# Linear attention and a squared-ReLU layer on one core: aligned tiles, u from one row, the bonus moved by SBUF transfers, new engine orders

## The chip, the core and the metric

The kernel runs on one core of one Trainium2 chip. The core has five engines with instruction streams of their own: TensorE (PE; its weight loads are listed as PEld), VectorE (DVE), ScalarE (ACT), GpSimd (POOL) and SyncE (SP), which here only issues DMAs. Tiles lie in SBUF, 128 partitions wide; PE writes to PSUM, eight banks of 2 KB in each partition. Sixteen DMA engines move data. The metric is the device time of one execution in microseconds (us), as the median of several runs.

## The reference

A linear attention with a decayed state for 4 batches, 8 heads, 768 positions and 48 channels, then a layer with squared ReLU on 3072 tokens of 384 channels:

```
for t in range(S):
    cur = np.einsum('bhd,bhe->bhde', u[None] * kt, vt)
    y[:, :, t] = np.einsum('bhd,bhde->bhe', rt, state + cur)
    state = wt[:, :, :, None] * state + np.einsum('bhd,bhe->bhde', kt, vt)
...
x = attn_out.transpose(0, 2, 1, 3).reshape(B * S, H * D)
h = x @ w_in                 # 384 x 2048
r = np.maximum(h, 0.0)
return ((r * r) @ w_out)     # 2048 x 384
```

The term with u, the bonus, touches one position alone: it adds to y at t the row v at t, times the sum over d of r, u and k.

## The kernel before

The 3072 tokens are cut into 12 steps of 256 (three to a batch). A step's tile holds 128 partitions with two neighbouring positions each (j = 0, 1) for all 8 heads; the 128 partitions are two chunks (c = 0, 1) of 64. Each step goes through these operations, each a small function:

- **Loads** (`ld`): w, r, k, v of a step, 384 KB each, in runs of 384 bytes. The weights come as eight pieces of 768 KB and are cast to bf16 (`cast`). u is loaded as 128 equal rows (`load_u`, L188).
- **Decays**: `ww_` multiplies the two positions' w (L243), `lw_` takes the logarithm on ACT (L247), `cum_` sums along the positions on PE (L284 to L287), `exp_` and `ac_` go back on ACT (L291, L298). `rw_` and `kw_` make further products on DVE or POOL (L256, L260).
- **Decayed r and k**: `rd_` on DVE (L305); their transposes by PE (`tr_`, L314) and a copy (`rkt_`, L323) in steps 0 to 3, by DMA (`dtr_`, L326) from step 4 on.
- **Inside a chunk**: `p_` multiplies r and k (L341), `pm_` masks on DVE (L351 or L354), `y_` multiplies by v (L394).
- **State**: `su_` (L371), `ts_` (L379, L381) and `sn_` on POOL (L386); `yc_` adds the state's part to y (L394).
- **Bonus**: `ku_` and `qp_` on POOL form u k r (L264, L269), `q_` sums it on DVE (L273), `vq_` on POOL multiplies v by it and writes bf16 (L277). `yq_` (L411) adds it to y on PE: a 64-row product with the matrix `spread` for each of the two positions j and the two chunks c. The rows of y in PSUM are ordered by (j, position in the chunk) with the chunk in the free dimension, those of `vq` by (c, position) with j in the free dimension, so the product moves rows.
- **y on to the layer**: `ysb_` copies y from PSUM to bf16 on ACT or DVE (L436). Its transpose `xT` is made by PE and a copy (`yt_`, L444, `xt_`, L449) in steps 0 to 5, by DMA (`dyt_`, L453) from step 6 on.
- **Layer**: `m1_` (L464), eight groups of six matmuls a step; `rl_` (ReLU, on ACT L473 or DVE L475); `sq_` (square, L481 or L483); `m2_` (L489), two halves of 16 matmuls, in four pieces each; `os_` scales out of PSUM (L496, L498); `store` (L502).

What sets the order of the work is the text `ORDER` (L17): one word for each operation, with its step, for some the PSUM bank after a colon and the engine after an equals sign (A, V, G for ACT, DVE, POOL). The program is issued in this order, and each engine, and SP's DMA queue, executes its own instructions in it. `warm_` words are products without use at the start (L506).

PSUM is held as two double banks `att` for the attention part, two banks `bk` for `m2_` and transposes, and two banks `m1_bank` for `m1_`. Tiles in SBUF come from rotating pools; `half_ones` has 4 bytes in a partition, `q` 64, and a head's part of `r_raw` and `k_raw` 576.

Of the kernel before, what the change touches and what calls it, by code (L numbers as in the profile page):

```python
# [17 lines left out]
ld.0.w warm_.16.0 ld.1.w ld.0.k ld.0.u ld.0.r ld.1.r ww_.1=V ww_.0=V ld.1.k ld.0.v lw_.0 lw_.1 kw_.0=V  # L18
cum_.1:0 ku_.0 cum_.0:1 ld.0.i warm_.13.0 ac_.0 ac_.1 rw_.0=V exp_.0 qp_.0 ld.1.v exp_.1 rd_.0.0 rd_.0.1
tr_.0.0:0 ld.1.i warm_.1.1 rw_.1=V ld.2.w rkt_.0.0=A tr_.0.1:1 q_.0 ku_.1 rkt_.0.1=A ld.3.i rd_.1.0  # L20
p_.0.0:mm v_.0=A kw_.1=V qp_.1 warm_.2.0 rd_.1.1 su_.0:1 ld.2.k tr_.1.0:0 pm_.0.0 ts_.0.0=A tr_.1.1:1
rkt_.1.0=A p_.0.1:0 sn_.0.0 ld.2.r pm_.0.1 rkt_.1.1=A vq_.0 v_.1=A ts_.0.1=V y_.0:0 q_.1 cast.i.0=A sn_.0.1
p_.1.1:mm yq_.0 pm_.1.1 yc_.0 vq_.1 p_.1.0:1 ysb_.0=A ld.2.i warm_.3.0 pm_.1.0 ld.0.o cast.i.1=A yt_.0:0
su_.1:0 xt_.0=V y_.1:1 ts_.1.0=V ld.1.o yq_.1 ww_.2=V m1_.0.2:0 sn_.1.0 m1_.0.3:1 rl_.0.2=A yc_.1 cast.i.3=V
rl_.0.3=A m1_.0.1:0 lw_.2 ts_.1.1=V ld.2.o ysb_.1=A m1_.0.6:1 sq_.0.1=V ld.2.v cum_.2:0 rl_.0.1=V rl_.0.6=A
yt_.1:1 exp_.2 m1_.0.7:1 xt_.1=V rw_.2=V m1_.0.0:0 rl_.0.7=A kw_.2=V rl_.0.0=A rd_.2.0 m1_.1.0:1 cast.i.2=G
ac_.2 m1_.1.7:0 sq_.0.3=A rl_.1.0=V tr_.2.0:0 rd_.2.1 ku_.2 ld.3.o rl_.1.7=A m1_.1.5:1 sq_.0.0=A ld.3.w
m1_.0.5:0 rl_.1.5=V ld.3.r tr_.2.1:1 cast.o.0=V sn_.1.1 rl_.0.5=A m1_.1.4:1 rkt_.2.0=V m1_.0.4:0 rl_.1.4=A
rkt_.2.1=A rl_.0.4=V qp_.2 m1_.1.1:1 sq_.1.2=V m2_.0.0.0:0 cast.o.1=A m1_.1.2:0 ld.3.k pp_.2:10 rl_.1.2=A
m2_.0.0.1 rl_.1.1=A pm_.2.1 v_.2=G sq_.0.2=A m1_.1.3:0 cast.o.2=G ld.3.v q_.2 m1_.1.6:1 m2_.0.1.0:1 pm_.2.0  # L30
rl_.1.6=A vq_.2 m2_.0.1.1 cast.o.3=A ld.4.w rl_.1.3=V su_.2:0 m2_.0.1.2 ww_.3=G sq_.1.0=A ld.4.r m2_.0.0.2
lw_.3 m2_.0.1.3 sq_.1.1=A cum_.3:1 os_.0.1=V ld.4.k m2_.0.0.3 rw_.3=V exp_.3 m2_.1.0.0:1 ts_.2.0=V kw_.3=G
sq_.1.3=A rd_.3.0 m2_.1.0.1 ld.5.r sn_.2.0 m2_.1.0.2 ac_.3 os_.0.0=A rd_.3.1 m2_.1.0.3 v_.3=A ku_.3
store.0.1 tr_.3.0:0 os_.1.0=V yy_.2:01 ww_.4=V qp_.3 ld.4.v rkt_.3.0=V lw_.4 tr_.3.1:1 ysb_.2=A m2_.1.1.0:0
rkt_.3.1=V ld.5.k ts_.3.0=A cum_.4:1 rw_.4=V sn_.3.0 yt_.2:1 exp_.4 m2_.1.1.1 xt_.2=V ac_.4 ld.5.w m2_.1.1.2
rd_.4.0 kw_.4=G m1_.2.1:1 ts_.3.1=V dtr_.4.0 ku_.4 m1_.2.0:0 rd_.4.1 rl_.2.1=A rl_.2.0=A m1_.2.5:1 q_.3
dtr_.4.1 pp_.3:01 sn_.3.1 rl_.2.5=A m1_.2.3:0 pm_.3.1 ld.6.w vq_.3 m2_.1.1.3 rl_.2.3=A pm_.3.0 m1_.2.2:1
v_.4=A qp_.4 m1_.2.6:0 ld.7.w sq_.2.0=A rl_.2.2=V yy_.3:10 rl_.2.6=V ld.5.v sq_.2.1=A ww_.5=V kw_.5=G
os_.1.1=A m1_.2.4:1 rw_.5=V ld.7.r ysb_.3=A m1_.2.7:0 lw_.5 yt_.3:1 ts_.4.0=V rl_.2.4=A m2_.2.0.0:0 ld.6.k
xt_.3=A sn_.4.0 sq_.2.2=V m2_.2.0.1 ku_.5 cum_.5:0 store.1.1 m2_.2.1.0:1 ac_.5 q_.4 exp_.5 m1_.3.1:1  # L40
ts_.4.1=V rl_.2.7=A m2_.2.1.1 rd_.5.0 rl_.3.1=A m1_.3.7:0 ww_.6=G sq_.2.3=A rd_.5.1 m2_.2.1.2 dtr_.5.0
# [12 lines left out]
cum_.8:1 rw_.8=G sq_.5.0=A m1_.5.2:1 ld.10.w m2_.4.0.0:1 rl_.5.2=V rl_.5.4=A ww_.9=G m2_.4.0.1 exp_.8
ts_.7.1=V qp_.7 m1_.5.7:0 ac_.8 rd_.8.0 sq_.5.1=A m1_.5.6:1 rd_.8.1 m2_.4.0.2 dtr_.8.0 rw_.9=G m2_.4.0.3
# [34 lines left out]
def kernel(  # L90
# [17 lines left out]
    C = 128  # L108
# [458 lines left out]
```

## Time and profile before

| What | us |
|---|---|
| median of 3 runs (lowest, highest) | 189.27 (189.17, 189.53) |
| the profiled execution: span | 186.7 |
| busy PE, DVE, ACT, POOL | 177.0, 125.8, 125.1, 104.9 |
| L464 (`m1_`), 576 matmuls | 74.3 |
| L489 (`m2_`), 384 matmuls | 71.9 |
| L394 with `spread` (`yq_`), 48 matmuls | 6.0 |
| `vq_` on POOL, mean of 12 | 1.520 |
| `ysb_`, mean: ACT x9, DVE x3 | 0.796, 0.958 |
| `ku_`, `qp_` on POOL, mean of 12 | 1.878, 1.910 |

The span is the time from the first to the last instruction that the profile shows; the runs' times have some us more around it. Groups are listed by source line, engine and operation, with the names of the tiles written and read; their busy time is a union, while a mean of matmuls counts overlapping ends. A DMA's time runs from its issue to its landing.

### The profile page before, as it was taken

The page shows a single profiled execution, that of the slowest core. Times are in us where ns is not written, and L with a number is a line of the kernel's source. Part 1 is how long each engine was busy: PE and PEld are TensorE (multiplying, and loading weights), DVE is VectorE, ACT ScalarE, POOL GpSimd, SP SyncE. Part 2 cuts the span into 40 slices and gives each one's busy share as a digit, 9 for nine tenths or more (in the row PEclk, how much of TensorE's full clock was granted, in tenths as well). Part 3 has the DMA queues.
Part 4 walks back from the last instruction along what each step waited for, and adds up shares of the span by engine and source line. Part 5 has one row for each costly group of instructions (what it writes and reads, how often), then busy time and mean ns, then how long its engine had stood idle before and what let it go on. Part 6 is the DMA issues. An engine that isn't in the chain of part 4 may idle for free.

```text
span 186.7 us, 5422 instructions
## 1 busy us (share of the span) xinstructions
PE 177.0 (95%) x2303; PEld 125.4 (67%) x2303; DVE 125.8 (67%) x170; ACT 125.1 (67%) x205; POOL 104.9 (56%) x99
## 2 busy tenths in 40 slices
PE   7686998999999999999999999999999999999992
PEld 2344587766777777777776766777666777776761
DVE  4379979686799876983849699795946472562020
ACT  5278978889659795797687577968541656156732
POOL 7289627695897998959496981563934130000000
PEclk9999999999999999999999999999999999999999
DMA  6999999999999999979999999890539150203022
GB/s 151 269 274 341 330 280 381 340 280 264 275 234 218 257 239 236 248 148 147 279 185 260 220 270 251 240 147 32 66 63 201 30 172 0 46 0 126 4 84 84
DMA packets 78952, 35.81 MB, mean 192 GB/s; under 512 B 72144, under 2 KB 77392, under 8 KB 78928
## 3 DMA queue, kind: packets, MB, share of 16 engines
q1 hardware_dynamic: 78928, 35.46, 82.5%
q8 instruction: 18, 0.29, 0.7%
q14 instruction: 6, 0.05, 0.1%
HBM read 25.36 MB, written 4.72 MB: 161 GB/s over the span
## 4 chain that ended last, share of the span: by engine, by line
PE 80%; DVE 8%; ACT 5%; issue 3%; DMA 3%; SPq 0%; ACTq 0%
PE m L464 32%; PE bk L489 31%; PE att L394 8%; DVE rdec_buf L305 4%; PE att L341 3%; PE att L371 3%; DMA w_raw<-in_w_dram 3%; PE bk L444 1%; PE att L286 1%; PE att L287 1%; ACT att L291 1%; DVE r_raw L256 1%; ACT ac_buf L298 1%; DVE pmT L351 1%; DVE pmT L354 1%
## 5 line engine op out<-in xcount | busy, mean ns | idle before, releaser
L464 PE MATMUL m<-xT,wi_sb 128*128 128x256 bf16 x576 | 74.3, 273 | 0.5 <-ACT gt L473 0.5
L489 PE MATMUL bk<-wo_sb,gt 128*128 128x384 bf16 x384 | 71.9, 326 | 0.0
L464 PEld LDWEIGHTS <-wi_sb 128*128 128x128 bf16 x576 | 54.9, 98 | 13.9 <-issue 1.4
L473 ACT ACTIVATE gt<-m 128x512 f16<-128x512 f32 x68 | 39.7, 596 | 34.4 <-PE m L464 34.1
L489 PEld LDWEIGHTS <-gt 128*128 128x128 bf16 x384 | 36.9, 98 | 19.3
L481 ACT ACTIVATE gt<-gt 128x1024 bf16<-128x1024 f16 x36 | 37.6, 1053 | 0.9 <-DVE gt L475 0.7
L354 DVE TENSOR_TENSOR pmT<-att,mask 128x1024 bf16<-128x1024 f32 x22 | 26.3, 1218 | 5.6 <-PE att L341 5.5
L386 POOL TENSOR_TENSOR S<-t_state,ac_buf 128x384 bf16<-128x384 f32 x20 | 18.7, 935 | 19.9 <-DVE t_state L381 13.2
L475 DVE TENSOR_SCALAR gt<-m 128x512 f16<-128x512 f32 x28 | 19.2, 687 | 14.6 <-PE m L464 11.9
L264 POOL TENSOR_TENSOR ku<-k_raw,u_bc 128x768 f32<-128x768 f32 x12 | 22.5, 1878 | 9.1 <-DVE q L273 4.7
L269 POOL TENSOR_TENSOR ku<-ku,r_raw 128x768 f32<-128x768 f32 x12 | 22.9, 1910 | 1.0 <-DMA r_raw<-in_r_dram 0.8
L277 POOL TENSOR_TENSOR vq<-v_raw,q 128x768 bf16<-128x768 f32 x12 | 18.2, 1520 | 9.1 <-DVE q L273 4.8
L305 DVE TENSOR_TENSOR rdec_buf<-r_raw,att 128x768 bf16<-128x768 f32 x12 | 11.3, 952 | 3.8 <-ACT att L291 2.2
L498 DVE TENSOR_SCALAR o_sb<-bk 128x384 f32<-128x384 f32 x11 | 6.1, 551 | 11.0 <-PE bk L489 11.0
L291 ACT ACTIVATE att<-att 128x768 f32<-128x768 f32 x12 | 9.4, 795 | 3.7 <-PE att L287 3.6
L305 DVE TENSOR_TENSOR rdec_buf<-k_raw,att 128x768 bf16<-128x768 f32 x12 | 11.4, 947 | 0.5 <-ACT ac_buf L298 0.5
L506 PE MATMUL bk<-warm 128*128 128x512 bf16 x35 | 10.5, 452 | 1.2 <-DVE half_ones L212 1.2
L273 DVE TENSOR_REDUCE q<-ku 128x16 f32<-128x768 f32 x12 | 11.3, 943 | 0.0
L496 ACT ACTIVATE o_sb<-bk 128x384 f32<-128x384 f32 x13 | 6.4, 490 | 6.2 <-PE bk L489 6.2
L483 DVE TENSOR_TENSOR gt<-gt 128x1024 bf16<-128x1024 f16 x12 | 8.9, 753 | 2.0 <-ACT gt L473 2.0
L381 DVE TENSOR_TENSOR t_state<-S,att 128x384 f32<-128x384 bf16 x16 | 8.7, 546 | 1.8 <-PE att L371 1.8
L247 ACT ACTIVATE lw_buf<-ww 128x384 bf16<-128x384 f32 x12 | 6.2, 524 | 5.3 <-DVE ww L243 5.3
(72 smaller groups left out, 179.8 us busy)
## 6 DMA issues: line engine op xcount, KB each, us to landing
w_raw<-in_w_dram SPq DMA_DIRECT2D x12, 384.0 KB, 5.1
k_raw<-in_k_dram SPq DMA_DIRECT2D x12, 384.0 KB, 6.1
r_raw<-in_r_dram SPq DMA_DIRECT2D x12, 384.0 KB, 6.2
v_raw<-in_v_dram SPq DMA_DIRECT2D x12, 384.0 KB, 6.0
out_dram<-o_sb SPq DMA_DIRECT2D x24, 192.0 KB, 3.1
w_st<-in_moe_w_in_dram SPq DMA_DIRECT2D x4, 768.0 KB, 8.5
w_st<-in_moe_w_out_dram SPq DMA_DIRECT2D x4, 768.0 KB, 8.7
rkT<-rdec_buf SPq DMA_TRANSPOSE x16, 4.0
```

The costliest lines, as they stand in the source:

```text
L264: nc.gpsimd.tensor_mul(ku[:], raw["k", s][:, :, 1:3, :], u_bc[:, :, None, :].to_broadcast([C, H, 2, D]))
L269: nc.gpsimd.tensor_mul(ku[:], ku[:], raw["r", s][:, :, 0:2, :])
L277: nc.gpsimd.tensor_mul(vq[:].rearrange("p j h d -> p h j d"), raw["v", s][:], tiles.pop(("q", s))[:, :, :, None].to_broadcast([C, H, 2, D]))
L305: nc.vector.tensor_mul(rdec[:, i, :, :, 0:D], x.rearrange("p h j d -> p j h d"), cs[:, i, 0:DM].rearrange("p (h d) -> p h d", h=H)[:, None ...
L354: nc.vector.tensor_mul(pmT, ps_p[:].rearrange("p e (a x) -> p (e a) x", a=2), mk.to_broadcast([C, 4, 2 * C]))
L386: nc.gpsimd.tensor_mul(t[:], tiles.pop(("ts", s, c))[:].rearrange("p (a e d) -> p a e d", a=HP, e=2), tiles["a_c", s][:, :, c, :, None].to ...
L394: nc.tensor.matmul(ps_y[rows, c, cols], lhsT, rhs, start=fresh, stop=True, skip_group_check=True)
L464: nc.tensor.matmul(ps1[:, j, :], wi_sb[:, n // 4, kk, n % 4 * 128:(n % 4 + 1) * 128], tiles["xT", s][:, :, kk, :], start=(kk == 0), stop=( ...
L473: nc.scalar.activation(rl, m1, AF.Relu, scale=RS)
L475: nc.vector.tensor_scalar(out=rl, in0=m1, scalar1=RS, scalar2=0.0, op0=ALU.mult, op1=ALU.max)
L481: nc.scalar.activation(gt, rl, AF.Square)
L489: nc.tensor.matmul(m2, gt[:, n, c * C:(c + 1) * C], wo_sb[:, n, :], start=(n == 0), stop=(n == NT - 1))
```

## The change

Four things change at once.

1. **Tiles.** The pools are replaced by fixed lists of tiles, handed out and returned in the order of use by `buf(kind, ...)`. Their number for each kind stays (4 for w, r, k, v; 2 or 3 for most others; 6 for S; 4 for `xT`; 3 for `gt`). Their sizes are multiples of 128 bytes: `half_ones` is cut from 64 columns, `q` from 32 floats, and the heads of r and k stand 640 bytes apart, k's first one 64 bytes in. The tiles of `os_` are cut from a weight stage that has become free. In PSUM the four single banks are one list `one`, for `m1_`, `m2_` and transposes alike.
2. **u.** One row is loaded, a product with a row of ones spreads it over 128 partitions in PSUM (`ub_`, in f32), and ACT copies it (`uc_`).
3. **Bonus.** In steps 3 to 11 there is no `yq_`. Four DMAs (`mv_`) on SP's queue move the rows of `vq` to the rows that y has, and `ysb_` becomes an addition on DVE.
4. **Order.** All of `ORDER` is new: the order on each engine, the banks, and which engine does `rl_`, `sq_`, `os_`, `ww_`, `rw_`, `kw_`, `v_`, `cast`, `rkt_`, `ts_`, `xt_`. By number, `rl_` on ACT and DVE goes from 68 and 28 to 63 and 33, `os_` from 13 and 11 to 20 and 4; `warm_` products go from 35 to 29. The transposes by DMA stay in the same steps.

```diff
 ORDER = """
-ld.0.w warm_.16.0 ld.1.w ld.0.k ld.0.u ld.0.r ld.1.r ww_.1=V ww_.0=V ld.1.k ld.0.v lw_.0 lw_.1 kw_.0=V
-cum_.1:0 ku_.0 cum_.0:1 ld.0.i warm_.13.0 ac_.0 ac_.1 rw_.0=V exp_.0 qp_.0 ld.1.v exp_.1 rd_.0.0 rd_.0.1
-tr_.0.0:0 ld.1.i warm_.1.1 rw_.1=V ld.2.w rkt_.0.0=A tr_.0.1:1 q_.0 ku_.1 rkt_.0.1=A ld.3.i rd_.1.0
-p_.0.0:mm v_.0=A kw_.1=V qp_.1 warm_.2.0 rd_.1.1 su_.0:1 ld.2.k tr_.1.0:0 pm_.0.0 ts_.0.0=A tr_.1.1:1
-rkt_.1.0=A p_.0.1:0 sn_.0.0 ld.2.r pm_.0.1 rkt_.1.1=A vq_.0 v_.1=A ts_.0.1=V y_.0:0 q_.1 cast.i.0=A sn_.0.1
-p_.1.1:mm yq_.0 pm_.1.1 yc_.0 vq_.1 p_.1.0:1 ysb_.0=A ld.2.i warm_.3.0 pm_.1.0 ld.0.o cast.i.1=A yt_.0:0
-su_.1:0 xt_.0=V y_.1:1 ts_.1.0=V ld.1.o yq_.1 ww_.2=V m1_.0.2:0 sn_.1.0 m1_.0.3:1 rl_.0.2=A yc_.1 cast.i.3=V
+warm_.10.0 ld.0.u ld.0.w ld.1.w ww_.0=V ub_:3 ww_.1=V ld.0.k ld.0.r ld.1.r lw_.0 ld.1.k cum_.0:1 rw_.0=V kw_.0=G lw_.1
+uc_=A exp_.0 rd_.0.0 rd_.0.1 rw_.1=V warm_.4.4 ku_.0 kw_.1=V warm_.4.3 cum_.1:0 ac_.0 ld.0.v exp_.1 qp_.0 tr_.0.0:0
+tr_.0.1:3 rkt_.0.0=A warm_.6.1 warm_.1.5 rd_.1.1 ld.1.v rd_.1.0 rkt_.0.1=A p_.0.0:n pm_.0.0 ku_.1 v_.0=A ac_.1
+p_.0.1:1 su_.0:0 ts_.0.0=A q_.0 tr_.1.0:0 ld.3.i tr_.1.1:2 pm_.0.1 warm_.3.3 warm_.1.3 sn_.0.0 y_.0:1 yc_.0 ld.1.i
+ld.2.w vq_.0 v_.1=A yq_.0 rkt_.1.1=A cast.i.3=A ld.0.i ts_.0.1=V rkt_.1.0=V p_.1.1:m ysb_.0=A yt_.0:0 su_.1:0 pm_.1.1
+p_.1.0:1 xt_.0=V m1_.0.6:2 cast.i.1=A sn_.0.1 qp_.1 ww_.2=G ts_.1.0=V ld.2.r m1_.0.3:3 m1_.0.2:1 sn_.1.0 m1_.0.7:0
...
+dtr_.4.1 dtr_.5.0 rl_.3.3=V p_.4.0:1 p_.4.1:0 pm_.4.1 pm_.4.0 dtr_.5.1 m2_.1.1.1 m1_.3.0:0 m2_.1.1.2 store.1.0
+m2_.1.1.3 ld.6.r q_.5 y_.4:0 su_.5:1 rw_.6=V sq_.2.0=A lw_.6 rl_.3.5=A rl_.3.0=A ww_.7=G sn_.4.1 mv_.4 yc_.4 ld.7.r
+ld.6.v sq_.3.0=A os_.1.1=A m1_.3.7:1 m2_.2.0.0:3 ts_.5.0=V sq_.2.1=A sq_.2.3=A rl_.3.7=A sq_.3.2=A vq_.5 ku_.6 qp_.6
+rw_.7=G ysb_.4 p_.5.1:1 p_.5.0:0 kw_.6=G m2_.2.1.0:0 pm_.5.0 m2_.2.1.1 yt_.4:1 ld.8.k cum_.6:0 m2_.2.1.2 exp_.6
...
 """
+MOVED = range(3, 12)
...
+    kinds = dict(
+        w=(4, [C, H, 2, D], FP32), r=(4, [C, 1280], FP32), k=(4, [C, 1312], FP32), v=(4, [C, H, 2, D], FP32),
...
+    for kind, first in (("r", 0), ("k", 16)):
+        free[kind] = [t[:, first:first + H * 160].rearrange("p (h x) -> p h x", h=H)[:, :, 0:3 * D].rearrange(
+            "p h (n d) -> p h n d", n=3) for t in free[kind]]
...
     def load_u():
-        nc.sync.dma_start(
-            out=u_bc[:],
-            in_=bass.AP(tensor=u.tensor, offset=u.offset,
-                        ap=[[0, C]] + [list(x) for x in u.ap]))
+        nc.sync.dma_start(out=u_row[0:1, :],
+                          in_=bass.AP(tensor=u.tensor, offset=u.offset, ap=[[0, 1]] + [list(x) for x in u.ap]))
+
+    def ub_():
+        tiles["ub"] = one[int(slot["ub_",])]
+        nc.tensor.matmul(tiles["ub"][:, 0:DM], ones_row[0:1, :], u_row[0:1, :], start=True, stop=True)
+
+    def uc_():
+        copy = nc.scalar.copy if where["uc_",] == "A" else nc.vector.tensor_copy
+        copy(u_bc[:].rearrange("p h d -> p (h d)"), tiles["ub"][:, 0:DM])
...
-    half_ones = consts.tile([C, 2], BF16)
+    half_ones = consts.tile([C, 64], BF16, name="half_ones")[:, 0:2]
...
+    def mv_(s):
+        vq, vqt = buf("vq", s), buf("vqt", s)
+        for c in range(2):
+            for j in range(2):
+                nc.sync.dma_start(out=vqt[j * Q:(j + 1) * Q, c, :],
+                                  in_=vq[c * Q:(c + 1) * Q, j].rearrange("p h d -> p (h d)"))
...
     def ysb_(s):
-        y_sb = tiles["ysb", s] = a_mid.tile([C, 2, DM], BF16, name="y_sb")
-        copy = nc.scalar.copy if where["ysb_", s] == "A" else nc.vector.tensor_copy
-        copy(y_sb[:], tiles.pop(("y", s))[:, :, 0:DM])
+        ps_y, y_sb = tiles.pop(("y", s))[:, :, 0:DM], buf("y_sb", s)
+        if s in MOVED:
+            nc.vector.tensor_add(y_sb[:], ps_y, buf("vqt", s)[:])
+        else:
+            (nc.scalar.copy if where["ysb_", s] == "A" else nc.vector.tensor_copy)(y_sb[:], ps_y)
```

## The prediction

> **What bounds the kernel now.** I read the busy shares and the slices first, then the table by stage, the chain of waits of the first 25 us, and TensorE's timeline around one step of the attention part.
>
> ```profile
> PE 177.0 (95%) x2303; PEld 125.4 (67%) x2303; DVE 125.8 (67%) x170; ACT 125.1 (67%) x205; POOL 104.9 (56%) x99
> PE   7686998999999999999999999999999999999992
> DMA  6999999999999999979999999890539150203022
> ```
>
> TensorE (PE) is full from the sixth slice on; the DMA engines are full for the first two thirds and then not. Ends of matmuls are modelled, so "busy" alone proves little; the stages say more.
>
> ```profile
> 10.00:20.00 10.00, 7.46 (x146) 4.55 (x143) 9.47 (x13) 7.98 (x12) 9.03 (x7) 1.00 1.13 312
> 40.00:60.00 20.00, 19.89 (x298) 14.05 (x297) 15.83 (x23) 15.69 (x26) 16.79 (x13) 1.00 1.19 248
> 140.00:160.00 20.00, 20.00 (x298) 14.54 (x297) 11.47 (x14) 9.84 (x15) 4.61 (x4) 1.00 0.44 95
> ```
>
> The columns are the window, its length, busy us of PE, weight load, DVE, ACT and POOL, the granted clock, the DMA share and GB/s. From 40 us on no stage lacks more than 0.5 us of PE, at clock 1.00. Before 20 us PE is not the bound: DVE is at 9.47 of 10. The chain of waits shows how the first product comes about:
>
> ```profile
> 1.26 4.94 DMA w_raw<-in_w_dram
> 11.05 1.82 DVE rdec_buf L305 x2
> 17.72 1.14 DVE pmT L354
> 23.45 1.42 PE m L464 x12
> 177.50 5.86 PE bk L489 x36
> ```
>
> The first product of the feed-forward part (L464) starts at 23.45 us and the last of L489 ends at 183.36: 159.9 us in which PE is the bound. Around it lie 23.45 us of start and 3.3 us of tail (186.7 - 183.36). So an edit counts if it takes PE work out of the 159.9, brings 23.45 nearer, or opens a gap in PE.
>
> **The bonus products.** `yq_` in steps 3 to 11 goes: 4 matmuls a step, 36 in all. Their cost is read from start to start:
>
> ```profile
> 117.58 0.56 PE L394 MATMUL att<-v_bf,pmT 64*128 64x48 bf16 x32
> 117.98 0.48 PE L394 MATMUL att<-vq,spread 64*128 64x384 bf16 x4
> 118.39 0.53 PE L394 MATMUL att<-S,rkT 128*64 128x96 bf16 x16
> ```
>
> From 117.98 to 118.39 is 0.41 us for four. At 22.97 to 23.39 it is 0.42; I take 0.417. 9 x 0.417 = **3.75 us off PE**, inside the 159.9. Not more: the group's 320 ns a matmul counts overlapping ends.
>
> **What comes in its place.** `mv_` issues 4 DMAs a step on the SP queue, 36 in all, each 64 rows of 768 B (48 KB), and `ysb_` becomes a DVE addition of the moved tile. The addition: a DVE copy of the same tile took 958 ns, an addition of half the columns with the same kinds of operands 546 ns (L381), so 0.96 to 1.09; I take 0.96. Nine of these are 8.6 us of DVE, in place of six ACT copies of 0.80 and three DVE copies of 0.96. The transfer itself: there is no plain SBUF transfer in the trace. The nearest rows are
>
> ```profile
> out_dram<-o_sb SPq DMA_DIRECT2D x24, 192.0 KB, 3.1
> rkT<-rdec_buf SPq DMA_TRANSPOSE x16, 4.0
> xT<-y_sb SPq DMA_TRANSPOSE x6, 3.3
> ```
>
> and a store has landed in as little as 1.8 us, a transpose in as much as 6.9. So 1.8 to 6.9 us; I take 3.1, as a plain copy of more bytes. An issue takes SP 0.42 us where the queue is free and 1.2 and more where it is full (L161: 0.42 to 3.0); four at 0.55 are 2.2 us, so 5.3 us from the product `vq` to a tile that can be added. The Trainium skill, SBUF — State Buffer, section "The DMA setup-cost knee", says that a transfer pays about 2 us that do not depend on its size; by that, an estimate for 48 KB is 2.1 us, and the move would take 4.3. No row here shows such a transfer alone.
>
> Is it covered? I add up PE's work along the order text, with the groups' mean start-to-start times. `mv_` stands 1.8 us (step 4), 2.6 (step 10), 5.5 (step 11) and 6.5 to 14.5 (the other six) of PE work ahead of its `ysb_`, but `vq_` stands 6.9 and 3.1 earlier still in steps 4 and 10, and SP can start before its place in the text. The transposes or `yt_` that follow have another 1.4 to 7 us until the step's first L464. I leave steps 4 and 10 uncovered by 0.45 us each: **+0.9 us**, with bounds of 0 and 9 x 1.0.
>
> **The start.** The DMA engines work the loads off in turn: w, w, k with u, r, r, k; their packets end at 3.6, 5.0, 6.9, 8.7, 10.2 and 11.7 us, and a use starts some 1.2 us later. Loading one row of u instead of 128 takes 128 packets of 81 ns on 16 engines away, 0.65 us; issuing it first costs one SP issue of 0.46. That leaves r about 0.2 earlier. `ww_.0` no longer waits for the second w (6.22; now about 5.2), so exp is ready before r. The first L305 comes at 10.5 instead of 11.05. From there to the copy `xt_.0` DVE works without a break in both. Before, it runs to 22.97. Taken out ahead of `xt_.0` are q_.1 (0.86 us a step of the timeline) and pm_.1.0 (1.13); put in is rkt_.1.0 (0.68): -1.3 us. Together -1.85; the other engines (PE, ACT casts, vq on POOL at 17.4) come within 0.5 us of that, and I take **-1.3 us**, bounds 0 and -2.2. The one-row product `ub_` in f32 has no row here; bounds are the 0.16 us of a bf16 product of 384 columns and four times the cold 512-column product's 0.45, 1.8 us. It lies behind warm products, with ACT's use of it due only at 7.8, and I take nothing; at 1.8 it would push exp_.0 past the landing of r by less than 0.3.
>
> **Tiles at multiples of 128 bytes.** The 4-byte `half_ones`, the 64-byte `q` and heads of 576 B put most tiles off such multiples before. PE cannot gain: L464's matmuls follow each other every 109 ns at clock 1.00 whichever tile they read. For DMAs: the 384-byte packets of the first w load took 22 ns almost throughout, those of the second, in the same kind of tile, 27 on average, so the slow ones are not slow by place. Bounds: 0, and all at 22 ns, (27 - 22) x 64 packets an engine x 7 loads = 2.2 us of the start. I take 0. The Trainium skill, DMA: Bandwidth & Descriptors, section "How a descriptor splits into AXI transactions", has a transfer that starts off a boundary pay for extra beats; an estimate by its count, 13 beats against 12, is a twelfth of a load, some 0.1 us each, and the sum would be 0.5 us lower. The trace does not show it.
>
> **The orders.** Words moved between engines, at the groups' means: DVE 131 to 134 us, ACT 132 to 127, POOL 103 to 108, all under PE's 163. That products and sums may now use any of the four single banks costs nothing; L464 waited 0.5 us in all for its banks before. Products other than `yq_` stay as many; 35 warm products become 29, in idle time. Cost 0, with bounds from the rivals.
>
> **Sum**, on the profiled execution: 186.7 - 3.75 - 1.3 + 0.9 = 182.55. The median of the runs is 189.27, 2.6 above the span; 182.55 + 2.6 = 185.15, rounded to **185.1 us**.
>
> **Rivals.** (1) *SP becomes the bound, slower.* SP executes in order, and `mv_` waits for POOL's `vq_` with loads, transposes and stores behind it. Between 40 and 120 us SP spent 67.4 of 80 us issuing, 12.6 free. Seven of the nine moves, 28 issues, fall there. The last load of v was issued some 10 us before its use. So PE waits once 28 issues take over 22.6 us, 0.81 each, and the gain of 4.2 is gone at 0.96 each. At 1.1, between a free and a full queue, it is 30.8 - 22.6 = 8.2 us of waiting: 193.3. For it: full queues until 125 us. Against: SP's long issues are waits for the DMA engines, which the moves load by 36 x 64 packets on 79,000. (2) *The other engines become the bound.* Up to 60 us of PE work DVE now has 66.1 us to do, ACT 62.8, POOL 62.5; before 62.8, 59.2, 53.4. DVE's 62.8 were some 90% of the time it had. If nothing is spare, PE waits 3.3 us: 188.4. (3) *Better start*: the loads gain the whole 2.2 us and the moves are covered: 185.1 - 0.9 - 2.2 + 0.5 = 182.5. (4) *It does not do what it says*: where PE did `yq_` it now stands as long, waiting for the addition (3.75 instead of 0.9 us), and r's landing sets the start as before (1.3): 185.1 + 2.85 + 1.3 = 189.25.
>
> **Chances.** Forecast 0.50, (1) 0.19, (2) 0.13, (3) 0.12, (4) 0.06. The likeliest is 185.1; its own range is 183.3 to 187. The range over all, 182.0 to 191.0, takes in (2), (3) and (4) and the part of (1) up to 0.99 us an issue. What a measurement of this kernel can tell is about 0.2%, 0.38 us: faster 0.75, same 0.06 (rival 4), slower 0.19.
>
> **What would show it.** Right: the spread product in 12 matmuls instead of 48; the first L464 near 22.2; PE without gaps over 0.5 us from there to the end, and 156 us between the first and the last product. Wrong: waits of the addition on a DMA into the moved tile, or waits of PE for it; SP's issues of moves over 0.8 us; waits on `r_raw` or `w_raw` after 40 us; a first L464 at 23.4 or later.

## The result and the profile after

The changed kernel takes 196.57 us (median of 4 runs, 195.44 to 197.29), the kernel before 189.22 beside it: 1.0385 times as long, interval 1.0344 to 1.0425. Forecast were 185.1 us. Here and below, only executions less than 1.5% above the fastest of their kernel are counted, since single executions, of the kernel before too, come out some per cent longer; seven of the runs have one or two of these, and two of the seven, whose profile is of one, have no first product and stretch in the table. The page of the changed kernel shows, under busy time and slices:

```profile
PE 176.7 (90%) x2261; PEld 125.9 (64%) x2263; DVE 136.1 (70%) x172; ACT 121.0 (62%) x199; POOL 110.0 (56%) x105
PE   7867899959998997999993999799999999999992
PEclk9969999999999999999999799999999999999999
DMA  5999999993299979998697896963805944002033
```

TensorE has hardly less busy time although 36 products are gone (177.0 us before). Its row (40 slices of 4.9 us) has gaps in the ninth, sixteenth, twenty-second and twenty-sixth slice, and the granted clock, 9 throughout before, dips twice. The table by stage (window, its length, busy PE, weight load, DVE, ACT and POOL, clock, DMA share, GB/s) answers to the one shown of before:

```profile
10.00:20.00 10.00, 7.02 (x104) 4.83 (x108) 9.79 (x12) 6.51 (x12) 5.56 (x4) 0.83 1.08 360
40.00:60.00 20.00, 17.95 (x240) 13.09 (x238) 16.89 (x23) 17.58 (x25) 15.25 (x13) 1.00 0.70 201
140.00:160.00 20.00, 19.82 (x301) 14.98 (x300) 15.12 (x20) 13.79 (x21) 5.69 (x5) 1.00 0.51 106
```

Between 40 and 60 us TensorE lacks 2.05 us where it lacked 0.11. From 10 to 20 us the clock is 0.83. The chain of waits of the changed kernel (start, us, what) shows the first product and the worst place later:

```profile
3.35 4.84 DMA r_b<-in_r_dram
8.22 2.12 DVE r_b L283
12.25 1.92 DVE r_b L283
23.36 2.78 PE one L477 x24
103.11 2.83 DMA xT_b<-y_sb_b
```

r is there at 8.22 us, against 10.16 before, but the two products r times w (`rw_`, L283) take 2 us each, and the first product of the layer (L477, before L464) comes at 23.36, as before (23.39). The last product ends at 191.75. So the stretch from the first product of the layer to the last has grown from 159.97 to **168.38 us**, where 157.1 were forecast (159.97 - 3.75 + 0.9).

### The profile page after: what moved, and what is told of

It is laid out like the page before. It is cut to its first block, busy times and chain, and to the rows that moved or that the text cites. A ratio compares the mean times of both kernels' runs of the same rounds, so it can differ in the third digit from the quotient of the medians.

```text
span 195.5 us, 5424 instructions
## 1 busy us (share of the span) xinstructions
PE 176.7 (90%) x2261; PEld 125.9 (64%) x2263; DVE 136.1 (70%) x172; ACT 121.0 (62%) x199; POOL 110.0 (56%) x105
## 4 chain that ended last, share of the span: by engine, by line
PE 62%; DVE 16%; DMA 6%; issue 5%; ACT 4%; SPq 3%; POOL 1%; DVEq 0%; POOLq 0%; ACTq 0%
PE one L500 28%; PE one L477 24%; DVE rdec_buf L336 5%; PE att L414 4%; DMA r_b<-in_r_dram 2%; DVE r_b L283 2%; PE att L369 2%; DVE q_b L298 2%; DMA vqt_b<-vq_b 2%; DMA xT_b<-y_sb_b 1%; PE att L391 1%; DVE pmT_b L377 1%; ACT att L322 1%; DVE pmT_b L380 1%; SPq L352 1%
## 5 line engine op out<-in xcount | busy, mean ns | idle before, releaser
L477 PE MATMUL one<-xT_b,wi_sb 128*128 128x256 bf16 x576 | 72.3, 274 | 5.0 <-DMA xT_b<-y_sb_b 3.2
L500 PE MATMUL one<-wo_sb,gt_b 128*128 128x384 bf16 x384 | 70.8, 330 | 1.2 <-ACT gt_b L484 1.1
L477 PEld LDWEIGHTS <-wi_sb 128*128 128x128 bf16 x576 | 55.1, 98 | 16.8 <-DMA xT_b<-y_sb_b 3.4
L484 ACT ACTIVATE gt_b<-one 128x512 f16<-128x512 f32 x63 | 36.8, 596 | 32.3 <-PE one L477 31.6
L500 PEld LDWEIGHTS <-gt_b 128*128 128x128 bf16 x384 | 37.4, 99 | 22.9 <-issue 2.2
L492 ACT ACTIVATE gt_b<-gt_b 128x1024 bf16<-128x1024 f16 x35 | 35.9, 1052 | 0.2
L405 POOL TENSOR_TENSOR S_b<-t_b,ac_buf 128x384 bf16<-128x384 f32 x20 | 17.9, 893 | 30.6 <-DVE t_b L401 17.1
L380 DVE TENSOR_TENSOR pmT_b<-att,mask 128x1024 bf16<-128x1024 f32 x22 | 26.2, 1215 | 9.7 <-PE att L369 9.7
L295 POOL TENSOR_TENSOR ku_b<-ku_b,r_b 128x768 f32<-128x768 f32 x12 | 22.3, 1856 | 6.0 <-DMA r_b<-in_r_dram 5.7
L486 DVE TENSOR_SCALAR gt_b<-one 128x512 f16<-128x512 f32 x33 | 21.9, 683 | 4.6 <-PE one L477 4.4
L290 POOL TENSOR_TENSOR ku_b<-k_b,u_bc 128x768 f32<-128x768 f32 x12 | 24.3, 2027 | 1.2 <-DMA vqt_b<-vq_b 1.2
L506 ACT ACTIVATE w_st_b<-one 128x384 f32<-128x384 f32 x20 | 9.7, 488 | 17.7 <-PE one L500 17.4
L494 DVE TENSOR_TENSOR gt_b<-gt_b 128x1024 bf16<-128x1024 f16 x13 | 13.8, 1078 | 0.0
L336 DVE TENSOR_TENSOR rdec_buf<-k_b,att 128x768 bf16<-128x768 f32 x12 | 11.3, 947 | 0.5 <-issue 0.2
L298 DVE TENSOR_REDUCE q_b<-ku_b 128x16 f32<-128x768 f32 x12 | 11.3, 942 | 0.0
L283 DVE TENSOR_TENSOR r_b<-r_b,w_b 128x384 f32<-128x384 f32 x7 | 8.4, 1206 | 2.6 <-DMA r_b<-in_r_dram 2.6
```

What stands on the lines that cost most here:

```text
L290: nc.gpsimd.tensor_mul(buf("ku", s)[:], buf("k", s)[:, :, 1:3, :], u_bc[:, :, None, :].to_broadcast([C, H, 2, D]))
L295: nc.gpsimd.tensor_mul(ku[:], ku[:], buf("r", s)[:, :, 0:2, :])
L298: nc.vector.reduce_sum(buf("q", s)[:], buf("ku", s)[:], axis=AX.X)
L336: nc.vector.tensor_mul(rdec[:, i, :, :, 0:D], x.rearrange("p h j d -> p j h d"), cs[:, i, 0:DM].rearrange("p (h d) -> p h d", h=H)[:, None ...
L380: nc.vector.tensor_mul(pmT, ps_p[:].rearrange("p e (a x) -> p (e a) x", a=2), mk.to_broadcast([C, 4, 2 * C]))
L405: nc.gpsimd.tensor_mul(buf("S", s + c, 1 - c)[:], buf("t", s, c)[:].rearrange("p (a e d) -> p a e d", a=HP, e=2), tiles["a_c", s][:, :, c, ...
```

## The experiments

"First" is the start of the layer's first product, "stretch" the time from there to the end of its last one, both in the profiled execution; the ratio is to the kernel before on the same chip, with its interval. Where an expectation names a run with 190.3 or 193.7 us, tiles_warm_pool and after_start_mended are meant. Some expectations call the layer with squared ReLU the expert layer.

| run | first | stretch | time, us (lowest, highest) | ratio |
|---|---|---|---|---|
| before | 23.39 | 159.97 | 189.22 (189.13, 189.53) | |
| after | 23.36 | 168.38 | 196.57 (195.44, 197.29) | 1.0385 [1.0344, 1.0425] |
| tiles_alone | 26.73 | 161.26 | 194.02 (193.10, 194.32) | 1.023 [1.0171, 1.0289] |
| old_order_old_places | 23.56 | 159.95 | 188.59 (188.37, 190.90) | 0.9988 [0.9958, 1.0017] |
| tiles_warm | 24.86 | 163.59 | 193.10 (192.31, 193.55) | 1.0191 [1.012, 1.0262] |
| tiles_warm_pool | 23.62 | 160.31 | 188.75 (188.46, 189.03) | not given |
| warm_pool_old_places | 24.05 | 159.98 | 189.53 (188.89, 189.89) | 1.0023 [0.9999, 1.0047] |
| fitted_start | 25.82 | 160.79 | 191.39 (191.03, 191.69) | 1.0125 [1.0071, 1.018] |
| fitted_start_old_places | 24.15 | 161.11 | 192.10 (190.33, 192.80) | 1.0145 [1.0058, 1.0231] |
| best_start_old_order | 22.16 | 165.88 | 191.98 (191.68, 193.14) | 1.0167 [1.0135, 1.0199] |
| best_start_old_places | 24.84 | 164.27 | 193.79 (193.50, 194.18) | 1.0256 [1.0228, 1.0284] |
| after_old_places | | | 198.23 (197.06, 199.30) | 1.0459 [1.0375, 1.0542] |
| moves_old_order | 24.99 | 174.86 | 204.65 (202.72, 205.45) | 1.0784 [1.0703, 1.0865] |
| new_order_no_moves | 23.52 | 164.83 | 194.21 (193.43, 195.00) | 1.0248 [1.0187, 1.0309] |
| moves_unread | 23.46 | 167.21 | 196.04 (195.97, 196.20) | 1.0373 [1.032, 1.0426] |
| sp_order_mended | | | 195.66 (195.06, 196.25) | 1.033 [1.022, 1.044] |
| moves_on_pool | 23.28 | 178.79 | 207.65 (207.29, 208.59) | 1.0971 [1.0895, 1.1047] |
| after_start_mended | 22.02 | 165.17 | 193.43 (192.74, 194.05) | 1.025 [1.0167, 1.0334] |
| start_mended_no_moves | 22.50 | 166.44 | 194.05 (192.72, 194.49) | 1.0253 [1.0216, 1.0291] |

### What the tile places do

**tiles_alone**: the changed code with the order of before, u loaded to 128 rows, no moves, all spread products.

```diff
-MOVED = range(3, 12)
+MOVED = ()
-        nc.sync.dma_start(out=u_row[0:1, :], ...
+        nc.sync.dma_start(out=u_bc[:], in_=... ap=[[0, C]] + ...
```

> The order of before, yq_ in every step, u as 128 rows; only the tiles (and the code that hands them out) are the new ones. Theory A (the new tiles speed up the load packets, and the new order wastes it): 384-byte packets at 22 to 23 ns instead of 26, first L464 some 1 us earlier than 23.45, 188.0 to 189.0 us. Theory B (the place of a tile changes nothing, as forecast): 189.2.

The packets did get faster: 384-byte packets took 26.3 ns on average before and 23.1 here, 22 at nine in ten. And the time rose by 4.4 us (189.63 beside it). The stage table shows where:

```profile
10.00:12.00 2.00, 1.27 (x6) 0.39 (x4) 1.80 (x2) 0.83 (x2) 1.92 (x2) 1.00 1.02 262
12.00:14.00 2.00, 1.24 (x16) 0.95 (x17) 2.00 (x3) 1.05 (x2) 2.00 (x2) 1.00 1.04 325
14.00:16.00 2.00, 1.07 (x18) 0.54 (x18) 2.00 (x3) 1.60 (x2) 1.92 (x2) 0.61 1.00 302
16.00:18.00 2.00, 2.00 (x26) 1.38 (x24) 1.97 (x3) 0.48 (x1) 0.73 (x2) 0.50 1.08 386
```

TensorE waits for more than a third of each of the first three windows and is granted half its clock from 14.5 us on, here until 24.7 us; the kernel before, busy 2.00 and 1.52 us in the first two of these windows, keeps 1.00. VectorE's timeline has one line that does not fit:

```profile
13.01 1.98 DVE L286 TENSOR_TENSOR r_b<-r_b,w_b 128x384 f32<-128x384 f32 x1
```

The same product took 0.55 us before, where GpSimd was waiting for k until 13.20. Here k is there, and GpSimd's `ku_.1` runs from 12.77 to 14.57. **old_order_old_places** is the control: the same with the old sizes.

```diff
-r=(4, [C, 1280], FP32), k=(4, [C, 1312], FP32) ... q=(3, [C, 32], FP32)
+r=(4, [C, H * 144], FP32), k=(4, [C, H * 144], FP32) ... q=(3, [C, 16], FP32)
-    half_ones = consts.tile([C, 64], BF16, name="half_ones")[:, 0:2]
+    half_ones = consts.tile([C, 2], BF16, name="half_ones")
```

> The run with the new tiles alone (194.0 us) with the tile sizes and places of before: what is left of the change is its code for handing out the buffers (the out tiles taken from a weight buffer that has been read, four single PSUM banks taken by number), with the order of before, u loaded to 128 rows and no moves. If the places are what lost 4.7 us there, this is the kernel before, 188.5 to 189.6 us, with 26 ns a packet, the first r near 10.1 us and no half clock. Rival: if the handing out of the buffers lost it, 193 to 195 us.

It is the kernel before in time. So in this order the places alone lost the 4.4 us, not the new handing out of buffers. In the changed kernel the same edit, **after_old_places**, goes the other way:

> The changed kernel with the tile sizes of before for r, k, q and half_ones, half_ones ahead of all, so that the loaded tiles stand off multiples of 128 bytes. Theory A: 384-byte packets go from 23.1 back to some 26 ns and loads land later where SP's queue is the bound: 198 to 200. Theory B: 196.5.

198.23 us, 1.7 above the changed kernel, though the intervals of the two ratios overlap, so that a gain by the new places is not shown here. A loss of 4.4 us by them is excluded: what they cost depends on the order.

### Why earlier loads lose, and whether it can be mended

**tiles_warm** is tiles_alone with `warm_.13.0` raised to `warm_.18.0` and `warm_.4.2` behind `tr_.0.1`.

> The run with the order of before and the new tiles alone (194.0 us), with nine more warm products on TensorE: 18 in place of 13 behind the first cumulative sums, and four more between the second set of transposes of step 0 and its first products. Nothing else is changed, and nothing of the computation. Theory C (the start is longer because TensorE stood idle from 11.3 us on, busy 1.27, 1.24 and 1.07 of 2 us in the windows from 10 to 16 us, and was then granted half its clock from 14.5 to 24.7 us): the clock stays at 1.00 through the start, the first product of the expert layer comes near 24.0 instead of 26.7 us, and the time is 190.7 to 191.8 us. Rival D (the order of before does not suit the earlier loads, and the clock only follows from that): the products before the first product of the expert layer come no earlier, and the time stays at 193.5 to 194.5 us.

The clock stayed at 1.00 in every window of the start and the first product came 1.9 us earlier. So the half clock made that part of the late first product. The time did not follow: 193.10 us is 4.3 above the kernel before beside it, where tiles_alone was 4.4 above. The stretch grew by 2.3 us, and behind waits of 1.77 and 0.73 us that end at 33.65 and 35.79 the clock was halved there, from 35.6 to 39.0 us:

```profile
36.00:38.00 2.00, 2.00 (x15) 1.67 (x14) 1.76 (x2) 1.28 (x2) 2.00 (x2) 0.50 1.12 334
```

That alone is some 1.7 us by estimate (half of 3.4). **tiles_warm_pool** adds

```diff
-rw_.1=V
+rw_.1=G
```

> The run before this one with the product r times w of step 1 on GpSimd instead of VectorE. Theory P (VectorE's product of two SBUF tiles stands still while GpSimd reads SBUF: 1.98 us for rw_.1 beside ku_.1 where 0.55 us is usual): VectorE gets back some 2 us there and GpSimd spends 1.0 us more, the first product of the expert layer comes 1 to 1.5 us earlier than in the run before this one, and the time is 189.2 to 190.8 us. Rival: the 2 us on VectorE are taken back by GpSimd's longer chain to vq_.0, and the time is within 0.4 us of the run before this one.

First product 1.2 us earlier, stretch 3.3 shorter, no half clock in it, and 188.75 us, the time of the kernel before (188.80 beside it), in the two counted executions of four. So the product that stood, with what followed from it, is the part that shows in the time. **warm_pool_old_places** takes the places back in this run:

> The run with nine more warm products and r times w of step 1 on GpSimd (190.3 us) with the tile sizes and places of before; nothing else is changed. If the earlier loads of the new places turn into time once the clock and the blocked product are out of the way, this is 0.5 to 2 us longer, 190.8 to 192.3 us. If they do not, since the path after the loads is set by the engines, it is 188.5 to 190.5 us.

189.53: with clock and standing product out of the way the new places bring the first product 0.4 us earlier (23.62 against 24.05). Whether the time gains by it, 188.75 against 189.53 us on two chips, the two counted executions do not settle. Three more starts by hand were tried. **fitted_start** has u by the one-row product and `rw_.0 rw_.1` ahead of GpSimd's work, **fitted_start_old_places** the same on old sizes.

> The order of before with the new tiles, u spread by the one-row product, and a start set by hand: both products r times w stand on VectorE before GpSimd has u, so that they lie beside none of its products, the exponential stands ahead of the two chunk factors on ScalarE, and warm products fill TensorE's waits. No moves. Theory C and P (the earlier loads gain as soon as VectorE's products lie beside no product of GpSimd and the clock stays at 1.00): first product of the expert layer at 22.3 to 23.0 us against 23.6 in the run with r times w of step 1 on GpSimd and 23.4 before, time 188.0 to 189.3 us. Rival D (the rest of the order gives it back, as it did with the warm products alone): 189.5 to 191 us.

> The run before this one with the tile sizes and places of before (q 64 bytes, r and k 5184 bytes a partition, the two-column constant 4 bytes). Nothing else is changed. Theory (the places speed the packets up, 23.1 against 26.3 ns for 384 bytes, and a start that is fitted to the loads turns that into time): 0.7 to 2 us longer than the run before this one, with the first r a microsecond later. Rival (the path is set by the engines and the places give nothing): within 0.4 us of it.

fitted_start missed: its first product is at 25.82, not 22.3. Its clock was 0.50 from 18.9 to 25.7 us, with TensorE busy 0.92 and 1.11 us in the windows from 16 to 20; its twin with 0.92 and 1.19 in the windows from 18 to 22 kept 1.00. The twin's median is 0.7 us longer, but its executions (190.33 to 192.80) lie on both sides of those of fitted_start, and the profiles differ by the half clock. The pair says nothing of the places. **after_start_mended** puts the same cures into the changed kernel:

```diff
-rw_.0=V kw_.0=G ... rw_.1=V warm_.4.4 ku_.0 kw_.1=V warm_.4.3 cum_.1:0
+kw_.0=G rw_.0=G ... rw_.1=G kw_.1=G warm_.4.4 ku_.0 warm_.4.3 cum_.1:0 warm_.6.3
```

> The changed kernel with the start alone mended: r times w of steps 0 and 1 and k times w of step 1 on GpSimd, ahead of its products with u, and six warm products more behind the second cumulative sums. Nothing else is changed. Theory P and C: no product of VectorE stands for 2 us any more, the clock stays at 1.00 from 11 to 15 us, the first product of the expert layer comes at 20.5 to 22.0 us instead of 23.4, and the time falls by about as much, to 194 to 195.5 us. Rival D: the stretch behind it takes it back, 196 to 197.5 us.

First product at 22.02 and 193.43 us, 3.1 less. Only 1.3 us of the difference of the profiles lies ahead of the first product; the stretch is 3.2 shorter, some 1.7 of it by the half clock from 106.9 us that does not come here. The stage table of this run:

```profile
10.00:12.00 2.00, 1.58 (x20) 1.16 (x20) 1.00 (x2) 0.85 (x3) 1.87 (x3) 1.00 1.17 325
12.00:14.00 2.00, 1.18 (x6) 0.34 (x4) 1.62 (x2) 1.98 (x3) 1.92 (x2) 1.00 1.08 393
```

VectorE has time to spare where it was full (9.79 of 10 us from 10 to 20) and the clock is 1.00. **best_start_old_order** joins this start to the order of before, **best_start_old_places** does so on old sizes.

> The new tiles, u by the one-row product, the mended start of the changed kernel (r times w and k times w of the first two steps on GpSimd, warm products in the waits), and from the first product of the expert layer on the order of before, with the first casts and products of the expert layer in the changed kernel's sequence (group 3, then 1, then 0) and the spread products kept. No moves. Theory (the start's gain is real and was lost only to the blocked products and the clock; the order of before keeps its 160 us): first product at 22.0 us, 160 to 161.5 us to the last, time 187.3 to 188.8 us, which is faster than before by 0.2 to 1%. Rival D (the order of before needs its own start and gives the 1.4 us back in the first two steps): first product at 22.0, 162 us or more to the last, 189 to 191 us.

> The run before this one with the tile sizes and places of before; nothing else is changed. If the places are worth something once the start is fitted, the time is 0.5 to 2 us above the run before this one; if the path is set by the engines alone, it is within 0.4 us of it.

The first product came at 22.16, and the stretch gave back 5.9 us against 159.97: rival D by the stretch, while 191.98 us is above D's 189 to 191. The profiled execution, 193.14 us, is the longest of six and has a half clock from 35.1 to 38.6 us; the other five are 1.0 to 1.5 us shorter. TensorE waits 0.74, 0.68, 1.31 and 0.73 us before products at 25.21, 30.50, 33.28 and 35.43. On this start the places are worth 1.8 us (191.98 against 193.79, six executions of each on one chip): this is the one pair in which they gain clear of the noise. No version was shown to be faster than the kernel before.

### What the moves and the new order do

**moves_old_order** is tiles_alone with `mv_` behind `vq_` and no `yq_` from step 3 on; **new_order_no_moves** is the changed kernel with `MOVED = ()`, `yq_` behind `yc_` and the copies on VectorE.

> The order of before on the new tiles, u as 128 rows; yq_ of steps 3 to 11 gives way to mv_ right behind vq_ and the addition on DVE. Theory Q (the moves' place on SP's queue is what costs): 2 us or more slower than tiles_alone, 191 to 194, with waits on the moved tile or of the transposes. Theory O (the new order of the engines costs, the moves do what was forecast): 3 us faster than tiles_alone, 185 to 186.

> The new order without mv_; yq_ back right behind yc_ in every step, the copy of y stays on DVE in steps 3 to 11. Theory Q: the gaps at y_sb of step 4 (2.3 us) and at the transposed y of step 6 (3.4) shrink or go, 3.75 us of products come back: 194 to 196.5. Theory O: the gaps stay and the products come on top: 199 to 200.5.

On the old order the moves cost 174.86 - 161.26 + 3.75 = 17.4 us in the stretch, some 5.1 of it by half clocks of 3.4 and 6.8 us. On the new one it is 168.38 - 164.83 + 3.75 = 7.3 us in the profiled executions; the ratios (1.0385 and 1.0248) give 2.6 + 3.75 = 6.3. And without them the new order has a stretch 4.9 us longer than before. TensorE's timeline of new_order_no_moves shows waits for ScalarE and VectorE, where the kernel before has none over 0.5 us behind its first product of the layer:

```profile
41.23 0.52 PE L394 MATMUL att<-v_bf_b,rdec_buf 64*128 64x96 bf16 x16 [0.98 <-ACT ac_buf L332]
43.84 0.81 PE L503 MATMUL one<-wo_sb,gt_b 128*128 128x384 bf16 x4 [1.08 <-ACT gt_b L487]
61.87 0.82 PE L480 MATMUL one<-xT_b,wi_sb 128*128 128x256 bf16 x6 [0.80 <-ACT gt_b L487]
74.52 0.42 PE L372 MATMUL att<-rkT_b 64*64 64x128 bf16 x16 [0.45 <-DVE y_sb_b L455]
```

**moves_unread** puts only the transfers back, read by nobody:

```diff
-            nc.vector.tensor_add(y_sb[:], ps_y, buf("vqt", s)[:])
+        (nc.scalar.copy if where["ysb_", s] == "A" else nc.vector.tensor_copy)(y_sb[:], ps_y)
```

> The run with the new order without moves (194.2 us: 48 spread products, copies on VectorE) with the 36 transfers of the bonus put back on SP at the changed kernel's places; what they write is read by nobody, and the spread products add the bonus as before. The output is whole. Theory S (the transfers cost because SP issues in order and everything behind them, loads and transposes, comes later): the time rises with the transfers alone, to 197 to 201 us, with empty stretches of TensorE that end at loads or transposes. Rival A (they cost because the addition waits for the bonus): with nobody waiting, the time stays at 193.5 to 195.0 us.

196.04: between the two expectations. The transfers cost 1.8 us with nobody waiting for them; the intervals of the two ratios do not overlap. SP's own timeline shows how, at the transpose of step 6's y: first without moves, then with unread ones, then in the changed kernel.

```profile
99.28 2.11 SPq L470 DMA_TRANSPOSE xT_b<-y_sb_b  x1
```

```profile
98.20 4.02 SPq L358 DMA_TRANSPOSE rkT_b<-rdec_buf  x1
102.32 1.23 SPq L470 DMA_TRANSPOSE xT_b<-y_sb_b  x1
```

```profile
96.98 2.34 SPq L180 DMA_DIRECT2D w_b<-in_w_dram  x1
99.41 3.60 SPq L352 DMA_TRANSPOSE rkT_b<-rdec_buf  x1
103.11 1.23 SPq L467 DMA_TRANSPOSE xT_b<-y_sb_b  x1
```

The addition that makes y was done at 98.74 in the changed kernel. Its transpose was issued 4.4 us later, behind a load and another transpose, and TensorE stood still, as its own timeline says:

```profile
105.99 1.29 PE L477 MATMUL one<-xT_b,wi_sb 128*128 128x256 bf16 x9 [3.15 <-DMA xT_b<-y_sb_b]
```

After it the granted clock was 0.50 from 106.9 to 110.3 us, by estimate 1.7 us more (half of 3.4). Together that is 4.9 of the 7.3 us. In step 4 the moves themselves were late (the changed kernel's timelines of SP, of VectorE and of TensorE):

```profile
60.09 6.30 SPq L352 DMA_TRANSPOSE rkT_b<-rdec_buf  x4
66.48 0.53 SPq L512 DMA_DIRECT2D out_dram<-w_st_b  x1
67.07 0.43 SPq L180 DMA_DIRECT2D r_b<-in_r_dram  x1
67.59 2.55 SPq L308 DMA_DIRECT2D vqt_b<-vq_b  x4
```

```profile
73.76 0.96 DVE L450 TENSOR_TENSOR y_sb_b<-att,vqt_b 128x768 bf16<-128x768 f32 x1 [0.95 <-issue]
```

```profile
74.77 0.42 PE L369 MATMUL att<-rkT_b 64*64 64x128 bf16 x16 [1.49 <-DVE y_sb_b L450]
```

`vq_.4` was ready at 60.57; SP was in four transposes until 66.39, and the last of the four moves landed at 73.58. The one wait that the profile itself puts down to the moves, 3.2 us of VectorE, is in step 11, up to 163.33 us, and TensorE had work throughout. **sp_order_mended** exchanges both places.

```diff
-dtr_.4.0 dtr_.4.1 dtr_.5.0 ... dtr_.5.1 ... sn_.4.1 mv_.4 yc_.4 ... dtr_.7.1 dyt_.6
+dtr_.4.0 dtr_.4.1 mv_.4 dtr_.5.0 ... dtr_.5.1 ... sn_.4.1 yc_.4 ... dyt_.6 dtr_.7.1
```

> The changed kernel with two places of SP's queue exchanged: the four transfers of step 4's bonus stand ahead of step 5's two transposes instead of behind them, and the transpose of step 6's y stands ahead of step 7's second transpose. Nothing else is changed. Theory S (a transfer or transpose is late because SP, which issues in order, is held at the ones ahead of it): the empty stretches of TensorE at 73 us (2.3 us together) and at 102.6 us (3.3 us) go for the most part, with them the half clock from 106.9 to 110.3 us (1.7 us lost), and the time is 190 to 193 us. Rival T (the transfers' own landing, 2.9 us each, or what produces their data is late): the stretches stay or move to the transposes that now stand behind, and the time is 195 to 198 us.

Rival T, as far as time goes: 195.66 us. This profile is of an execution of 200.06 us, and what it shows is shown for that one alone. The wait at 102.6 us is gone; one of 3.23 us, up to 79.07, stands where 1.49 stood. SP's timeline and the waits of this run:

```profile
66.38 3.33 SPq L311 DMA_DIRECT2D vqt_b<-vq_b  x4
69.81 2.64 SPq L355 DMA_TRANSPOSE rkT_b<-rdec_buf  x2
...
73.13 1.17 SPq L183 DMA_DIRECT2D r_b<-in_r_dram  x2
```

```profile
DVE r_b L286 <- DMA r_b<-in_r_dram: 4.2, 1, 4.2
```

Now the load of r for step 6 is issued at 73.13, not 67.07, and VectorE, which has `rw_.6` ahead of the sum of the state (`ts_`) and the addition that TensorE needs, waits 4.2 us for it. What was put forward put something back. **moves_on_pool** takes the moves off it altogether.

```diff
-                nc.sync.dma_start(out=vqt[j * Q:(j + 1) * Q, c, :],
+                nc.gpsimd.dma_start(out=vqt[j * Q:(j + 1) * Q, c, :],
```

> The changed kernel with the bonus's four transfers a step issued by GpSimd right behind the product that makes the bonus, instead of by SP at its later places. Nothing else is changed. Theory S (SP's queue is what makes the transfers and the transposes behind them late): SP is free of 36 issues of 0.6 to 0.9 us, the empty stretches at 73 and 102.6 us shrink, and the time is 189 to 193 us if GpSimd's issues cost it under 0.6 us each. Rival T (the transfers' way itself is what is late): the waits of the addition on the bonus stay at some 3 us in single steps and the time is 195 to 198 us. Where an issue costs GpSimd a microsecond or more, GpSimd becomes the late engine and the time is above 200 us, and the run tells nothing of SP.

Each issue held GpSimd for 0.52 us (the median of 36), under the 0.6 of the expectation, and still it took 207.65. The timelines of GpSimd and of VectorE:

```profile
118.17 2.09 POOL L311 DMA_DIRECT2D vqt_b<-vq_b  x4 [0.30 <-POOL vq_b L304]
120.27 1.01 POOL L290 TENSOR_TENSOR k_b<-k_b,w_b 128x384 f32<-128x384 f32 x1
...
122.97 3.55 POOL L293 TENSOR_TENSOR ku_b<-k_b,u_bc 128x768 f32<-128x768 f32 x2
```

```profile
120.14 9.92 DVE L497 TENSOR_TENSOR gt_b<-gt_b 128x1024 bf16<-128x1024 f16 x2
```

```profile
L497 DVE TENSOR_TENSOR gt_b<-gt_b x13: 674/681/9320, 48.3 to 190.7; 128x1024 bf16<-128x1024 f16 x13
```

The row holds two squares, and the last line has the shortest, median and longest of the thirteen in ns: the first of the two lasts 9.32 us, from 120.14 to 129.46, while GpSimd works without a break from 120.27 to 128.91, and the second 0.68. The run says little of SP and much of VectorE. **start_mended_no_moves** stands against after_start_mended:

> The changed kernel with its start mended (193.7 us) and without the moves: 48 spread products and copies on VectorE. Against it stands what the moves are worth in the changed kernel. Theory M (the waits that the moves bring, on SP's queue and on the bonus, cost more than the 3.75 us of products that they save): 191.3 to 192.6 us, with no half clock. Rival (with the start mended the moves come out even or gain): 193.4 to 196 us.

The rival holds: 194.05 us without the moves (ratio 1.0253), 193.43 with them (1.025). In these two profiles, which have no half clock, 3.75 us of products are saved and some 2.5 us more of waiting has come into the stretch (165.17 against 166.44), 2.49 of it before the product that waits for step 6's y. By the times the moves come out even.

## Why the prediction was wrong

Its sum was 182.55 us of span; measured are 195.5. The 12.95 us between them are: the start 1.3 (23.36 against 22.1), the new order 4.9, the waits and the half clock behind the moves 6.4 (7.3 against 0.9), the tail 0.4 (3.75 against 3.35 us). These shares are from one profiled execution of each kernel.

- **The bonus products, 3.75 us.** 12 spread products are left, as said. The saving was not seen in the time, since more waiting came with it.
- **"I leave steps 4 and 10 uncovered by 0.45 us each: +0.9 us."** This step failed, though not by its prices. The landing was 2.9 us (taken 3.1), the addition 0.954 (0.96), an issue 0.67 (24.1 us for 36; taken 0.55). What failed is "SP can start before its place in the text": SP reached step 4's moves 7 us after their data. In step 4 TensorE waited 1.49 us for the addition, in step 10 not as much as 0.45. The larger part is what the sum did not ask for: what stands behind the moves in the queue. The late transpose of step 6's y cost 3.15 us and the half clock after it, and moves_unread shows 1.8 us without any wait on the bonus. That a better order of the queue would take these waits away was tried once, in sp_order_mended, and not shown.
- **Rival (1), SP as the bound**, given 0.19, was right in its place and sign, not in its condition: it wanted 0.81 us an issue and more. At 0.67 SP had time enough in sum, but in order of issue it did not.
- **The start, -1.3 us.** With the cures the first product comes at 22.02 and 22.16, where 22.1 were worked out; but there r times w and k times w are on GpSimd, so this shows that the time can be had, not that each term was right. In the changed kernel it was given back to two things that the step did not name. These are the changed kernel's timelines of VectorE and of GpSimd:

```profile
8.22 2.11 DVE L283 TENSOR_TENSOR r_b<-r_b,w_b 128x384 f32<-128x384 f32 x1 [1.84 <-DMA r_b<-in_r_dram]
12.17 2.00 DVE L283 TENSOR_TENSOR r_b<-r_b,w_b 128x384 f32<-128x384 f32 x1
```

```profile
8.11 1.80 POOL L290 TENSOR_TENSOR ku_b<-k_b,u_bc 128x768 f32<-128x768 f32 x1
9.99 2.00 POOL L295 TENSOR_TENSOR ku_b<-ku_b,r_b 128x768 f32<-128x768 f32 x1
11.95 1.81 POOL L290 TENSOR_TENSOR ku_b<-k_b,u_bc 128x768 f32<-128x768 f32 x1
```

  Each product of VectorE ends 0.4 us after the product of GpSimd that it met (9.91 and 13.76). I costed VectorE's chain by durations from a kernel in whose start the two did not meet. The other is TensorE's idle time from 8.85 to 11.45 us, followed by half the clock from 11.3 to 14.7. The Trainium skill, SBUF — State Buffer, section "Who interferes with whom", says that an instruction of VectorE with two SBUF inputs and one of GpSimd that reads SBUF exclude each other; the trace agrees, with 2.11 and 2.00 us in place of 0.55. tiles_warm_pool tries it: with the product of step 1 taken off VectorE the first product of the layer comes 1.2 us earlier.
- **Tiles at multiples of 128 bytes, "I take 0".** The step "the slow ones are not slow by place" fell: on the new places nine packets in ten take 22 ns, as in the upper bound, and the mean is an eighth lower (23.1 for 26.3 ns), where the prediction's estimate by beats was a twelfth. I had allowed this to gain up to 2.2 us and nothing else. In the order of before it lost 4.4. The same two effects are seen there, and tiles_warm_pool, without either, is back at the time of before.
- **The orders, "Cost 0".** The new order's stretch without moves is 164.83 us, with a mended start 166.44, against 159.97. Rival (2), the other engines as the bound, priced this at 3.3 us and was given 0.13. Part of it can be read from the groups (columns: busy us, mean ns, idle before), of before and then of after:

```profile
L483 DVE TENSOR_TENSOR gt<-gt 128x1024 bf16<-128x1024 f16 x12 | 8.9, 753 | 2.0 <-ACT gt L473 2.0
L256 DVE TENSOR_TENSOR r_raw<-r_raw,w_raw 128x384 f32<-128x384 f32 x8 | 5.6, 701 | 2.0 <-DMA r_raw<-in_r_dram 2.0
```

```profile
L494 DVE TENSOR_TENSOR gt_b<-gt_b 128x1024 bf16<-128x1024 f16 x13 | 13.8, 1078 | 0.0
L283 DVE TENSOR_TENSOR r_b<-r_b,w_b 128x384 f32<-128x384 f32 x7 | 8.4, 1206 | 2.6 <-DMA r_b<-in_r_dram 2.6
```

  Squares take 1078 ns on average instead of 753, r times w 1206 instead of 701: VectorE meets GpSimd more often. Of the 20 products in these groups, three took over 0.1 us more than the shortest of their kind before and nine after, and all twelve end some 0.4 us (r times w) or 0.55 (squares) behind the end of an instruction of GpSimd. That this is what opens the four waits of the new order was not tried by itself and stays open.
- **The product for u**, two matmuls in f32, took 0.85 us from start to end of its place, between the bounds, and lay in idle time, as said.
- **Two figures do not follow from the sum itself.** The upper end of the range, 191.0, is 1.02 us an issue in rival (1), not 0.99, and the 156 us named as a sign leave out the 0.9 us of waiting that the sum has.

## What to carry to other kernels

In a kernel whose order is written out by hand, a faster transfer is not free: it changes which instructions run side by side, so work out for each edit of the loads what will then run together, and look for products of VectorE beside work of GpSimd and for TensorE's idle time ahead of the first real product. When work is taken off the bounding engine and put on an in-order queue, ask what stands behind it in that queue, not only when it is done itself. And put in one part of such a change at a time: here four parts together hid a first product that could come 1.4 us earlier, and an order that cost 4.9 us by itself.

## What the runs showed of the hardware

- A product of VectorE with both inputs in SBUF can stand through several instructions of GpSimd, not just the current one: a square that took 0.68 us in most cases took 9.32, and ended 0.55 us after the last of seven instructions of GpSimd that followed each other without a pause.
- Tiles of w, r, k and v whose runs of 384 bytes start at multiples of 128 bytes are written at 23.1 ns a packet on average, those of before at 26.3; in old_order_old_places it was 27.5.
- TensorE's clock fell to 0.50 for 3.4 us in the changed kernel, twice, behind idle stretches of 2.6 and 3.15 us; in moves_old_order it did not behind one of 2.87; in tiles_alone it did, for 10.2 us, though no idle stretch ahead of it was over 1.2. The Trainium skill, TensorE: Matmul & The Clock Gate, section "What's actually happening", has a free-running window of 3413 ns decide; the lengths agree with that, and a window that starts anywhere would explain why like stretches end unlike. But TensorE was busy for more than half of each stretch shown of tiles_alone, which an idle window does not cover; old_order_old_places, with 1.90, 1.24 and 1.13 us in the same three windows, kept 1.00. What share of busy time decides stays open.
- A DMA issued by GpSimd from SBUF to SBUF took it 0.52 us (the median of 36).
